# Tokens and w1 loaded in a set order, sixteen query buffers for the final tiles, squares kept in PSUM, fifth-group shifts on VectorE, another list order

## The chip, the cores and the metric

The kernel runs on one core of a Trainium2 chip. The metric is the device time of one execution in microseconds (us). Before the change three executions took 253.4, 253.51 and 253.84 us. The first part of the profile names the engines: PE is the matrix engine (TensorE), PEld its weight loads, which overlap it (94% and 57% of the span in before), DVE the VectorE, ACT the ScalarE, POOL the GpSimd, and SP the engine that here only issues transfers. The span of a profile is about 1.8 us shorter than the time of the same execution. Every execution here is the time of one core.

## The reference, cut to what matters

```python
S, D, F = 2048, 640, 1536
# A: short convolution of k, product with v, long convolution over the tokens, product with q
kv = shift_conv(k, shift_k) * v
y  = irfft(rfft(pad(kv)) * rfft(pad(ssm_k)))[:S] + kv * ssm_D
a  = q * y
# B: two MLPs on x = q, the first with shifts of four channel groups by +1, -1, +2, -2 tokens
h  = gelu(layernorm(x) @ w1)          # "mm1"
hs = shift_groups(h) @ w2             # "mm2"
x1 = x + hs
b  = x1 + gelu(layernorm(x1) @ w3) @ w4   # "mm3", "mm4"
g  = sigmoid((x * gate_w).sum(-1))
out = g * a + (1 - g) * b
```

Tokens are handled in 16 tiles of 128. The kernel computes the long convolution with matmuls and elementwise products (`unit`, `combine`, `final`); the products are DVE's main load.

## The kernel before

All operations are first recorded in a list, then placed in order by a list scheduler when the kernel is built, and then emitted engine by engine. Each engine works through its own list in order. The priorities are shifted by a table of some 340 constants found by search; another table gives other lists. Because helpers record the operations, many instructions share one line of source: here `L1021` is nearly every matmul, `L1002` DVE's two-input products and sums, `L1007` the one-input ones with scalars, `L1012` ACT. These are the parts that matter.

```python
    const("w1")
    P.dma(sp, w1, B_w1.rearrange("(c p) f -> p c f", p=128), early=True)
    const("w1x")     # the four 32-column ends of w1's groups, gathered by ACT
    act(w1x.rearrange("p c (g q) -> p c g q", g=4), w1.rearrange("p c (g q) -> p c g q", g=4)[:, :, :, 128:160], ACTF.Copy)
    ...
    def ln_math(l, t):
        s = {f: st[l, f][:, t:t + 1] for f in range(6)}
        ts(s[4], s[0], s[0], D ** -2.0, ALU.mult, ALU.mult, eng="pool")
        ts(s[3], s[1], s[4], 1e-5, ALU.subtract, ALU.add, eng="pool")
        pool_pow(s[5], s[3], neghalf[:, t:t + 1])
        ts(s[2], s[0], 1.0 / D, None, ALU.mult, eng="pool")
    ...
    def mm1(sc, k=None):
        for ft in range(5):
            pr = ps(1, "mm1")[:, 0:n]
            mm(pr, ...)                       # ft == 4: the fifth group, from w1x
            if ft < 4:
                act(hT[:, ft, 2 + t0:2 + t0 + n], pr, ACTF.Gelu_apprx_tanh)
            else:
                for g in range(4):            # four shifted gelus on 32 partitions each
                    c0, q = 2 + SHIFT[g] + t0, slice(32 * g, 32 * (g + 1))
                    act(hT[q, 4, c0:c0 + n], pr[q], ACTF.Gelu_apprx_tanh)
    ...
    def mm2(t):
        ...
        act(X[:, t, :].rearrange("p (b n) -> p b n", b=2), pr, ACTF.Copy, accum=st[1, 0][:, t:t + 1])
        act(xn2[t % 2], X[:, t, :], ACTF.Square, scale=D ** -0.5, accum=st[1, 1][:, t:t + 1])
    def ln2(t):
        ln_math(1, t)
        ts(xn2[t % 2], X[:, t, :], ...)                       # normalise
        P.dma(sp, xt[...], xn2[t % 2], transpose=True)        # DMA transpose
    ...
    def final(hh, c, q, k):
        qt, gy, ab = qb[k % 3], gyb[k % 6], abb[k % 4]        # three query buffers
        P.dma(sp, qt, rows(A_q))
        act(qt[:, 0], qt[:, 0], ACTF.Copy, scale=gst[3][:, ts_:ts_ + 1])
        ...
        tt(gy, gy, qt, ALU.mult)
        tt(gy, gy, two(X), ALU.add)
        P.dma(sp, rows(out), gy)
```

Only the sum of the squares is wanted, so the square's elements are junk. But they are written into `xn2[t % 2]`, the buffer that the DMA transpose of two tiles earlier still reads.

Of the kernel before, what the change touches and what calls it, by code (L numbers as in the profile page):

```python
# [494 lines left out]
def bass_gated_mix__ssm_conv_h3__mixer_s_mlp__prompt_kernel(  # L495
# [36 lines left out]
    def ps(n, cls):  # L532
# [3 lines left out]
    BIASES = {'combine-0-1|dve': -407794.3,  # L536
     'combine-0-2|dve': -45893.4,
     'combine-0-3|dve': -300815.7,
     'combine-1-1|dve': 387348.8,
     'combine-1-2|dve': 105422.5,  # L540
     'combine-1-3|dve': 217575.6,
     'const-G|sp': 262450.7,
     'const-Rh|sp': 136620.7,
     'const-R|sp': 305660.3,
     'const-d|act': 212132.6,
     'const-esel|act': -74065.4,
     'const-gelu|act': 205074.8,
     'const-gsum|act': -162352.0,
     'const-gsum|pe': -204554.3,
     'const-gw|act': -345180.8,  # L550
     'const-id|act': 44971.2,
     'const-set|dve': 264773.9,
     'const-shk|sp': 548954.8,
     'const-taps|act': -347541.8,
     'const-taps|pe': 157141.2,
     'const-w1x|act': -118397.4,
     'const-w1|sp': 86861.3,
     'const-w2|sp': -203887.8,
     'const-warm|dve': 531209.6,
     'const-warm|pe': -474841.2,  # L560
     'final-0-0-0-6|act': 471334.1,
     'final-0-0-0-6|dve': 95864.6,
     'final-0-0-0-6|pe': -207210.8,
     'final-0-0-0-6|sp': 33107.2,
     'final-0-0-1-7|act': 502462.3,
     'final-0-0-1-7|dve': -145429.9,
     'final-0-0-1-7|pe': -1657225.0,
     'final-0-0-1-7|sp': 36878.1,
     'final-0-1-0-4|act': -542556.9,
     'final-0-1-0-4|dve': 90833.3,  # L570
     'final-0-1-0-4|pe': -17806.8,
     'final-0-1-0-4|sp': 180740.8,
     'final-0-1-1-5|act': 162211.6,
     'final-0-1-1-5|dve': 299763.8,
     'final-0-1-1-5|pe': 53865.8,
     'final-0-1-1-5|sp': 517150.6,
     'final-0-2-0-2|act': 48931.5,
     'final-0-2-0-2|dve': 237254.9,
     'final-0-2-0-2|pe': 74789.6,
     'final-0-2-0-2|sp': 187724.9,  # L580
     'final-0-2-1-3|act': -58044.8,
     'final-0-2-1-3|dve': -198209.5,
     'final-0-2-1-3|pe': -447313.6,
     'final-0-2-1-3|sp': -178044.8,
     'final-0-3-0-0|act': -70783.7,
     'final-0-3-0-0|dve': 107510.8,
     'final-0-3-0-0|pe': -417546.4,
     'final-0-3-0-0|sp': 12746.7,
     'final-0-3-1-1|act': -75347.7,
     'final-0-3-1-1|dve': 217341.1,  # L590
     'final-0-3-1-1|pe': 46063.4,
     'final-0-3-1-1|sp': 295314.0,
     'final-1-0-0-14|act': 545361.7,
     'final-1-0-0-14|dve': -299052.3,
     'final-1-0-0-14|pe': -547102.0,
     'final-1-0-0-14|sp': -128720.9,
     'final-1-0-1-15|act': 283548.0,
     'final-1-0-1-15|dve': 287063.5,
     'final-1-0-1-15|pe': 74100.7,
     'final-1-0-1-15|sp': 55218.8,  # L600
     'final-1-1-0-12|act': 75127.8,
     'final-1-1-0-12|dve': 225694.6,
     'final-1-1-0-12|pe': -32443.2,
     'final-1-1-0-12|sp': 271002.4,
     'final-1-1-1-13|act': -378541.6,
     'final-1-1-1-13|dve': 60153.4,
     'final-1-1-1-13|pe': -4036185.1,
     'final-1-1-1-13|sp': -631105.6,
     'final-1-2-0-10|act': -55974.0,
     'final-1-2-0-10|dve': 51404.3,  # L610
     'final-1-2-0-10|pe': -1881219.8,
     'final-1-2-0-10|sp': 107741.8,
     'final-1-2-1-11|act': 24136.8,
     'final-1-2-1-11|dve': 51566.4,
     'final-1-2-1-11|pe': 130287.3,
     'final-1-2-1-11|sp': 52505.2,
     'final-1-3-0-8|act': -186216.5,
     'final-1-3-0-8|dve': 209149.2,
     'final-1-3-0-8|pe': -92431.9,
     'final-1-3-0-8|sp': -234054.7,  # L620
     'final-1-3-1-9|act': 328185.7,
     'final-1-3-1-9|dve': 118940.0,
     'final-1-3-1-9|pe': 182235.6,
     'final-1-3-1-9|sp': 183596.6,
     'gate|act': 43517.7,
     'gate|pool': -106208.4,
     'h_chunk-0|act': -159010.0,
     'h_chunk-0|pe': -40842.3,
     'h_chunk-1|act': 400527.7,
     'h_chunk-1|pe': 579587.5,  # L630
     'h_chunk-2|act': 221955.9,
     'h_chunk-2|pe': -278173.1,
     'h_chunk-3|act': -142551.9,
     'h_chunk-3|pe': -95219.8,
     'h_chunk-4|act': -295038.4,
     'h_chunk-4|pe': -117699.7,
     'h_fold-0|act': -43635.4,
     'h_fold-0|dve': -182917.2,
     'h_fold-0|sp': 128933.9,
     'h_fold-1|act': 131439.2,  # L640
     'h_fold-1|dve': -106402.2,
     'h_fold-1|sp': 76238.2,
     'h_fold-2|act': 54189.3,
     'h_fold-2|dve': 10793.0,
     'h_fold-2|sp': 183656.1,
     'h_fold-3|act': -176689.9,
     'h_fold-3|dve': -178738.7,
     'h_fold-3|sp': 510928.9,
     'h_fold-4|act': -169023.8,
     'h_fold-4|dve': 297432.5,  # L650
     'h_fold-4|sp': -174960.5,
     'h_load-0|sp': 509674.0,
     'h_load-1|sp': 167622.4,
     'h_load-2|sp': 13065.6,
     'h_load-3|sp': -76450.5,
     'h_load-4|sp': -69693.6,
     'kv_block-0-0|act': -236465.6,
     'kv_block-0-0|dve': -155765.4,
     'kv_block-0-0|pe': -216177.4,
     'kv_block-0-0|sp': 24500.6,  # L660
     'kv_block-0-1|act': 170890.0,
     'kv_block-0-1|dve': -229659.6,
     'kv_block-0-1|pe': 43906.6,
     'kv_block-0-1|sp': 205152.3,
     'kv_block-0-2|act': 125536.7,
     'kv_block-0-2|dve': -356717.8,
     'kv_block-0-2|pe': 79125.3,
     'kv_block-0-2|sp': 171049.0,
     'kv_block-0-3|act': 70834.6,
     'kv_block-0-3|dve': -219421.9,  # L670
     'kv_block-0-3|pe': 33243.5,
     'kv_block-0-3|sp': 114498.1,
     'kv_block-1-0|act': -172843.4,
     'kv_block-1-0|dve': -88259.4,
     'kv_block-1-0|pe': 310482.8,
     'kv_block-1-0|sp': 94105.8,
     'kv_block-1-1|act': -189736.4,
     'kv_block-1-1|dve': -311893.1,
     'kv_block-1-1|pe': 420317.8,
     'kv_block-1-1|sp': -113999.1,  # L680
     'kv_block-1-2|act': 257985.6,
     'kv_block-1-2|dve': 265069.2,
     'kv_block-1-2|pe': -186714.4,
     'kv_block-1-2|sp': -188963.0,
     'kv_block-1-3|act': -77752.5,
     'kv_block-1-3|dve': 217795.5,
     'kv_block-1-3|pe': -171943.0,
     'kv_block-1-3|sp': -97522.0,
     'ln1-0-1|act': -229928.8,
     'ln1-0-1|dve': 338936.6,  # L690
     'ln1-0-1|pe': -122227.5,
     'ln1-0-1|pool': -277023.9,
     'ln1-1-2|act': -121291.7,
     'ln1-1-2|dve': 34755.1,
     'ln1-1-2|pe': -464286.9,
     'ln1-1-2|pool': -2789.2,
     'ln1-10-12|dve': 135278.3,
     'ln1-10-12|pool': -82370.4,
     'ln1-10-12|sp': -519951.2,
     'ln1-12-14|dve': -149131.9,  # L700
     'ln1-12-14|pool': -189370.6,
     'ln1-12-14|sp': 129838.2,
     'ln1-14-16|dve': -273427.8,
     'ln1-14-16|pool': 348966.8,
     'ln1-14-16|sp': 511015.6,
     'ln1-2-3|act': 96809.9,
     'ln1-2-3|dve': 22463.4,
     'ln1-2-3|pe': -57286.1,
     'ln1-2-3|pool': -278158.0,
     'ln1-3-4|act': -17404.0,  # L710
     'ln1-3-4|dve': -2033735.8,
     'ln1-3-4|pe': -35392.7,
     'ln1-3-4|pool': 516069.5,
     'ln1-4-6|act': 23443.4,
     'ln1-4-6|dve': 371099.5,
     'ln1-4-6|pe': -141280.2,
     'ln1-4-6|pool': -37793.4,
     'ln1-6-8|act': 12616.8,
     'ln1-6-8|dve': 165383.0,
     'ln1-6-8|pe': 116177.6,  # L720
     'ln1-6-8|pool': -295203.5,
     'ln1-8-10|dve': -783165.6,
     'ln1-8-10|pool': 537697.9,
     'ln1-8-10|sp': -103863.4,
     'ln2-0|dve': 438689.5,
     'ln2-0|pool': 86456.1,
     'ln2-0|sp': 58318.2,
     'ln2-10|dve': -21795.2,
     'ln2-10|pool': -278895.9,
     'ln2-10|sp': -615162.9,  # L730
     'ln2-11|dve': 57754.3,
     'ln2-11|pool': -184196.2,
     'ln2-11|sp': 147086.4,
     'ln2-12|dve': -51938.1,
     'ln2-12|pool': -156601.3,
     'ln2-12|sp': -509388.8,
     'ln2-13|dve': 850852.2,
     'ln2-13|pool': -139798.1,
     'ln2-13|sp': 135197.4,
     'ln2-14|dve': 230784.7,  # L740
     'ln2-14|pool': -86117.4,
     'ln2-14|sp': 23549.2,
     'ln2-15|dve': -232737.1,
     'ln2-15|pool': 384762.2,
     'ln2-15|sp': 223053.3,
     'ln2-1|dve': -307987.6,
     'ln2-1|pool': 231749.2,
# [694 lines left out]
```

## Time and profile before

| | before |
|---|---|
| median of 3 runs | 253.51 us |
| span of the profiled execution | 250.5 us |
| PE, DVE busy | 94%, 89% of the span |
| first matmul of mm1 | 13.46 us |
| tiles 2 and 3 of the tokens landed | 5.48 and 6.06 us |
| w1 issued, landed | 4.12, 12.92 us |
| PE's last matmul ends | about 244.2 us |

Three lines of the page of before: its first part (busy us, share of the span, instructions), the clock granted to PE in 40 slices of the span (in tenths), and the chain of waits that ended last, by engine.

```profile
PE 236.6 (94%) x1564; PEld 143.4 (57%) x1564; DVE 223.0 (89%) x337; ACT 171.9 (69%) x327; POOL 73.0 (29%) x94
PEclk9999999999999999999999999999999999999998
PE 44%; DVE 17%; ACT 14%; DMA 11%; POOL 9%; issue 3%; SPq 1%; DVEq 0%; ACTq 0%; POOLq 0%
```

PE and DVE are both near the length of the span, PE is granted full speed up to the last slice (mean clock 0.996; in the clock's records half speed begins at 248.4 us), and the chain runs over PE most of the time.

The chain of waits of before between 119 and 134 us (start, us, what) shows a loop:

```profile
119.40 2.57 DMA arena<-arena
...
122.05 0.84 ACT arena L1012 x2
...
122.98 1.12 POOL arena L1007
...
124.17 1.66 POOL arena L1187
...
125.85 0.45 DVE arena L1007
...
126.33 2.67 DMA arena<-arena
...
129.08 0.84 ACT arena L1012 x2
```

A transpose ends, then the square that had to wait for its buffer runs, then POOL computes the power, DVE normalises, and the next transpose starts: seven microseconds a round, for a value that has nothing to do with the transpose.

From the groups of instructions by form of before (count, busy us, mean ns, idle time before and who ended it): the squares (with the w1x copy), the shifted gelus on 32 partitions, and POOL's statistics.

```profile
L1012 ACT ACTIVATE arena<-arena 128x640 bf16<-128x640 bf16 x17 | 12.6, 742 | 11.5 <-DMA arena<-arena 11.5
L1012 ACT ACTIVATE arena<-PSall 32x256 bf16<-32x256 f32 x16 | 6.0, 376 | 0.4 <-PE PSall L1021 0.2
L1012 ACT ACTIVATE arena<-PSall 32x512 bf16<-32x512 f32 x8 | 4.7, 589 | 0.1
L1007 POOL TENSOR_SCALAR arena<-arena 128x1 f32<-128x1 f32 x52 | 43.5, 839 | 48.0 <-ACT arena L1012 38.6 <-DVE arena L1184 7.3
```

ACT waits 11.5 us in all for transposes. A 128x1 operation of POOL takes 839 ns on average.

The timeline of PE of before, at the start (start, us, then what): twenty transposes, of the first four tiles of the tokens, come before mm1's first matmul.

```profile
11.16 1.84 PE L1228 MATMUL PSall<-arena 128*128 128x128 bf16 x20
13.46 6.11 PE L1021 MATMUL PSall<-arena 128*128 128x256 bf16 x70 [0.46 <-ACT arena L1012]
```

The timeline of SP of before at the end:

```profile
243.78 0.37 SPq L230 DMA_DIRECT2D arena<-in_A_q_dram  x1
```

The last query is loaded when PE is nearly done, since a buffer comes free only then.

To say where PE loses time I counted in each trace the columns that its matmuls move, divided them by 2,400 per us (a round figure just above the densest issue in these traces, 512 columns every 0.214 to 0.216 us) and took that from the time that went by. The count does not depend on how the profile models a matmul's end. The whole kernel moves 224.1 us' worth. In before 7.5 us are lost up to 30 us, 5.7 from there to 120, 3.8 between 120 and 150, 2.0 up to 240, and 7.4 after that.

### The profile page before, as it was taken

How to read it: one execution, taken by the hardware profiler on the slowest of the kernel's cores; microseconds unless marked ns; L12 is line 12 of the kernel's file. 1: busy time of each engine (PE TensorE's matmuls, PEld its weight loads, DVE VectorE, ACT ScalarE, POOL GpSimd, SP SyncE). 2: the span in 40 equal slices, each digit the busy share in tenths (PEclk: the TensorE clock that was granted, in tenths of full speed). 3: DMA queues.
4: the chain of work that ended last, by engine and by line, in shares of the span. 5: the costliest groups of instructions: out<-in, count | busy, mean ns of one | idle time of the engine just before them, and what ended most of it. 6: DMA issues, size and time to landing. Idle time of an engine off the chain costs nothing.

```text
span 250.5 us, 4194 instructions
## 1 busy us (share of the span) xinstructions
PE 236.6 (94%) x1564; PEld 143.4 (57%) x1564; DVE 223.0 (89%) x337; ACT 171.9 (69%) x327; POOL 73.0 (29%) x94
## 2 busy tenths in 40 slices
PE   7999999999999999999997979999999999999990
PEld 2488765455654575544474634676467645777750
DVE  5678889849999998898988899999999999998685
ACT  2699996999788999797724572236622286727993
POOL 1433199302460028855686722000000000000000
PEclk9999999999999999999999999999999999999998
DMA  6999999987799996596522210000000000303676
GB/s 141 366 275 274 286 220 231 229 183 208 118 236 263 293 244 161 132 309 137 141 38 43 52 26 3 0 13 16 0 0 3 1 0 3 106 0 104 167 198 188
DMA packets 59336, 33.87 MB, mean 135 GB/s; under 512 B 30136, under 2 KB 57652, under 8 KB 59316
## 3 DMA queue, kind: packets, MB, share of 16 engines
q1 hardware_dynamic: 57852, 33.50, 54.6%
q10 hardware_dynamic: 1464, 0.11, 0.4%
q8 instruction: 12, 0.20, 0.3%
q14 instruction: 8, 0.07, 0.1%
HBM read 24.42 MB, written 2.62 MB: 108 GB/s over the span
## 4 chain that ended last, share of the span: by engine, by line
PE 44%; DVE 17%; ACT 14%; DMA 11%; POOL 9%; issue 3%; SPq 1%; DVEq 0%; ACTq 0%; POOLq 0%
PE PSall L1021 43%; DVE arena L1002 15%; ACT arena L1012 14%; DMA arena<-arena 8%; POOL arena L1007 7%; DMA arena<-in_A_ssm_k_dram 2%; POOL arena L1187 2%; DVE arena L1007 1%; DMA arena<-in_A_q_dram 1%; SPq L230 1%; PE PSall L1228 1%; DVEq L443 0%; ACTq L443 0%; DVEq L441 0%; POOLq L441 0%
## 5 line engine op out<-in xcount | busy, mean ns | idle before, releaser
L1021 PE MATMUL PSall<-arena 128*128 128x320 bf16 (+4 forms) x1495 | 225.9, 311 | 5.9 <-ACT arena L1012 4.6
L1002 DVE TENSOR_TENSOR arena<-arena 128x640 bf16<-128x640 bf16 (+5 forms) x235 | 195.5, 881 | 13.2 <-ACT arena L1012 7.9
L1021 PEld LDWEIGHTS PSall<-arena 128*128 128x128 bf16 (+1 forms) x1495 | 138.4, 98 | 93.4 <-ACT arena L1012 9.6
L1012 ACT ACTIVATE arena<-PSall 128x640 bf16<-128x640 f32 (+8 forms) x206 | 121.5, 645 | 26.4 <-PE PSall L1021 21.6
L1007 POOL TENSOR_SCALAR arena<-arena 128x1 f32<-128x1 f32 (+2 forms) x61 | 46.2, 761 | 59.2 <-ACT arena L1012 39.7
L1012 ACT ACTIVATE arena<-arena 128x640 bf16<-128x640 bf16 (+4 forms) x55 | 34.5, 629 | 29.6 <-DVE arena L1002 15.8
L1012 ACT ACTIVATE arena<-PSall,arena 128x640 bf16<-128x640 f32 (+1 forms) x32 | 20.4, 660 | 16.8 <-PE PSall L1021 16.7
L1187 POOL TENSOR_TENSOR arena<-arena 128x1 f32<-128x1 f32 (+1 forms) x26 | 25.5, 984 | 1.6
L1007 DVE TENSOR_SCALAR arena<-arena 128x640 bf16<-128x640 bf16 (+1 forms) x37 | 14.5, 404 | 6.6 <-POOL arena L1187 6.2
L1183 DVE BATCH_NORM_STATS2 arena<-arena 128x6 f32<-128x320 bf16 x32 | 13.6, 476 | 3.9 <-DMA arena<-in_A_q_dram 3.9
L1047 PE MATMUL PSall<-arena 128*128 128x512 bf16 x24 | 7.9, 492 | 1.6 <-DVE arena L1043 1.6
L1002 POOL TENSOR_TENSOR arena<-arena 128x16 f32<-128x16 f32 x3 | 1.3, 447 | 18.0 <-DVE arena L1007 18.0
L1047 PEld LDWEIGHTS PSall<-arena 128*128 128x128 bf16 x24 | 2.7, 121 | 5.7 <-issue 3.2
L1228 PE MATMUL PSall<-arena 128*128 128x128 bf16 x40 | 3.2, 220 | 0.2
L1012 ACT ACTIVATION_READ_ACCUMULATOR arena<-PSall 128x1 f32 x16 | 3.3, 208 | 0.0
L1012 ACT ACTIVATION_READ_ACCUMULATOR arena<-arena 128x1 f32 x16 | 3.1, 195 | 0.0
L1050 ACT ACT_TABLE_LOAD x1 | 1.3, 1283 | 2.4 <-issue 2.4
L1228 PEld LDWEIGHTS PSall<-arena 128*128 128x128 bf16 x40 | 2.3, 97 | 1.0 <-DVE arena L1183 0.4
L1184 DVE BATCH_NORM_AGGREGATE arena<-arena 128x2 f32<-128x12 f32 x16 | 2.8, 196 | 0.0
L1043 DVE MEMSET arena<- 128x640 bf16 x1 | 0.6, 592 | 0.9 <-PEq L1427 0.9
L1141 DVE MEMSET arena<- 32x480 uint32 x2 | 0.9, 458 | 0.1
L1007 DVE TENSOR_SCALAR arena<-PSall 128x4 f32<-128x4 f32 x4 | 0.6, 146 | 0.1
(16 smaller groups left out, 2.0 us busy)
## 6 DMA issues: line engine op xcount, KB each, us to landing
arena<-in_A_k_dram SPq DMA_DIRECT2D x14, 400.0 KB, 4.6
arena<-in_A_q_dram SPq DMA_DIRECT2D x20, 160.0 KB, 2.9
arena<-in_A_ssm_k_dram SPq DMA_DIRECT2D x5, 512.0 KB, 5.5
arena<-in_A_v_dram SPq DMA_DIRECT2D x16, 160.0 KB, 3.6
out_dram<-arena SPq DMA_DIRECT2D x16, 160.0 KB, 2.4
arena<-in_A_q_dram SPq DMA_DIRECT2D x6, 320.0 KB, 9.2
arena<-in_B_w_dram SPq DMA_DIRECT2D x1, 1920.0 KB, 8.4
arena<-in_B_w_dram SPq DMA_DIRECT2D x1, 1152.0 KB
```

The lines of the kernel that those rows point to most:

```text
L230: fn = lambda e: e.dma_start(out, in_, **kw)
L1002: P.op(eng, lambda e: e.tensor_tensor(o, a, b, op), [a, b], [o], dve_ns(o, [a, b], 2) if eng == "dve" else 500)
L1007: P.op(eng, lambda e: e.tensor_scalar(o, real(a), s1, s2, op0=op0, **({} if op1 is None else {"op1": op1})), [a] + aps, [o], dve_ns(o, [a] ...
L1012: P.op("act", lambda e: e.activation(o, real(a), f, bias=bias, scale=scale, **({"accum_out": accum} if accum is not None else {})), [a] + ...
L1021: fns.append(lambda e, l=l, r=r, i=i: e.matmul(real(o), l, r, start=(i == 0), stop=(i == last)))
L1047: P.op("pe", [lambda e: e.matmul(real(pw), warm[:, 0:128], warm[:, 128:640], start=True, stop=True)] * 2, [warm], [pw], 856.0 if i < 4 els ...
L1050: P.op("act", lambda e: e.activation(tjunk[:, 1:2], ones[:, 0:1], ACTF.Gelu_apprx_tanh), [ones[:, 0:1]], [tjunk[:, 1:2]], 1700)
L1141: P.op("dve", lambda e: e.memset(kt[0:32, 0:3, :], 0.0), [], [kt[0:32, 0:3, :]], 500)
L1183: P.op("dve", lambda e, o=o, i=i: e.bn_stats(o, i), [i], [o], 400)
L1184: P.op("dve", lambda e: e.bn_aggr(bna[:, t, :], bns[k]), [bns[k]], [bna[:, t, :]], 120)
L1187: P.op("pool", lambda g: g.tensor_tensor(o, a, e, ALU.pow), [a, e], [o], 450 + 400 * n_of(o))
L1228: P.op("pe", [lambda e, c=c, pb=pb, xn=xn: e.transpose(real(pb)[:, 128 * c:128 * (c + 1)], xn[:, 128 * c:128 * (c + 1)], ident) for c in r ...
```

## The change

The intent is to take away the three losses: mm1's late start, the loop between squares and transposes, and the tail. The core of the diff (the table of priorities, some 370 lines, is cut):

```diff
     const("w1")
-    P.dma(sp, w1, ..., early=True)
+    P.dma(sp, w1, ..., bias=8e8, early=True)
     const("w1x")
-    act(w1x.rearrange("p c (g q) -> p c g q", g=4), w1.rearrange("p c (g q) -> p c g q", g=4)[:, :, :, 128:160], ACTF.Copy)
+    for g in range(4):
+        P.dma(sp, w1x[:, :, 32 * g:32 * (g + 1)], B_w1.rearrange("(c p) (g f) -> p c g f", p=128, g=4)[:, :, g, 128:160], bias=7.5e8, early=True)
     const("w2")                                   # likewise, bias 5e8 and 4e8
 ...
     def ln_math(l, t):
-        ts(s[4], s[0], s[0], D ** -2.0, ALU.mult, ALU.mult, eng="pool")
-        ts(s[3], s[1], s[4], 1e-5, ALU.subtract, ALU.add, eng="pool")
+        ts(s[2], s[0], 1.0 / D, None, ALU.mult, eng="pool")
+        ts(s[4], s[2], s[2], 1e-5, ALU.mult, ALU.subtract, eng="pool")
+        ts(s[3], s[1], s[4], None, ALU.subtract)            # on DVE
         pool_pow(s[5], s[3], neghalf[:, t:t + 1])
-        ts(s[2], s[0], 1.0 / D, None, ALU.mult, eng="pool")
 ...
-                P.dma(sp, X[:, i, :], A_q[0, 128 * i:128 * (i + 1), :], early=True)
+                P.dma(sp, X[:, i, :], A_q[0, 128 * i:128 * (i + 1), :], bias=(1e9, 9e8, 7e8, 6e8)[i], early=True)
 ...
             else:
+                hx = hxb[(2 * sc + (k or 0)) % 2][:, 0:n]
+                act(hx, pr, ACTF.Gelu_apprx_tanh)           # one gelu on 128 partitions
                 for g in range(4):
-                    act(hT[q, 4, c0:c0 + n], pr[q], ACTF.Gelu_apprx_tanh)
+                    P.op("dve", lambda e, o=hT[q, 4, c0:c0 + n], i=hx[q, :]: e.tensor_scalar(o, i, 1.0, None, op0=ALU.mult), ...)
 ...
-        act(xn2[t % 2], X[:, t, :], ACTF.Square, scale=D ** -0.5, accum=st[1, 1][:, t:t + 1])
+        act(pr, pr, ACTF.Square, scale=D ** -0.5, accum=st[1, 1][:, t:t + 1])
 ...
-        qt, gy, ab = qb[k % 3], gyb[k % 6], abb[k % 4]
+        qt, gy, ab = qb[k], gyb[k % 8], abb[k % 4]
 ...                                               # the last two tiles end in two halves
+        for e in ((0, 2),) if k < 14 else ((0, 1), (1, 2)):
 ...                                               # sixteen query buffers in oHF, free by then
-    BIASES = {...}
+    BIASES = {...}                                # other priorities: other list order
```

SP now issues, by these biases: tiles 0 and 1 of the tokens, w1, the four transfers of w1x, tiles 2 and 3, tiles 4 to 7, w2.

## The prediction

> **What bounds the kernel now.** By the first part of the page, over a span of 250.5 us, PE is busy 236.6 us (94%), DVE 223.0 (89%), ACT 171.9, POOL 73.0. Two engines limit it together: in the table of windows both are at or near 100% from 160 to 230 us. Counting the matmuls' moving columns in the trace, all but the warm-up makes 522 thousand; at the rate of the dense stretches (37 matmuls of 320 columns in 5 us) that is about 221 us, 224 with the small ones. So PE loses some 26 us, at three places:
> - start: mm1, which waits for tokens, w1 and w1x, starts at 13.5 us;
> - middle, 120 to 150 us: PE idles about 3 us. The chain of waits loops there: ACT square, POOL 1.1 to 2.9 us, POOL power 0.57, DVE 0.45, DMA transpose 2.6, back to ACT, since the square writes the buffer that the transpose reads. ACT waits 11.5 us in all for transposes;
> - tail: PE's last matmul ends near 244.2 us. The last query load is issued at 243.8, because only three query buffers exist, and takes 2.7 us; then scale, multiply, add, store.
>
> **Removed.** The squares' wait for transposes (they go to PSUM). From ACT: 24 shifted gelus on 32 partitions (10.7 us) and the w1x copy (0.7). From the tail: query loads and query scalings (0.56 each), which can run long before. From POOL's path after the square: all but the power. POOL ops stretch to 2.9 us while DVE runs two 1.44 us products[...].
>
> **Added or moved.** Six gelus on ACT (+2.8 us; net ACT -8.6). On DVE: 24 shifts, estimated 0.20 us (256 wide) and 0.28 us (512 wide) from its fixed cost of 0.11 to 0.15 us: 5.4 us; 16 subtractions of 128x1, 0.15 each: 2.4 us; the split of the last two tiles, 0.6 us. DVE grows about 8 us to 231, which eats a good part of the gain; it fits because most additions fall before 110 us, where DVE has idle time (about 5 us before 40 us, 4.4 from 40 to 60).
>
> **On the critical path.** Start: w1 is issued third instead of ninth; mm1 should begin at 10 to 11 us. But the taps and transposes done before it must still be done, and early mm1 is paced by ACT and DVE: net 1 to 2 us. Middle: 1 to 3 us, limited by DVE. Tail: 2 to 3 us (ACT per final falls from 1.8 to 1.25 us). The list order may win or lose 1 us. Sum about 7 us.
>
> **Predicted:** 246.5 us, 8 in 10 between 241.5 and 250.5. Faster by over 2%: 0.66; within 2%: 0.31; slower: 0.03.
>
> **What would show it right.** First mm1 matmul near 10.5 us. No wait of ACT for transposes. DVE busy 229 to 233 us, ACT 161 to 166. No query load after 230 us; at most 6 us from PE's last matmul to the end. DVE at least 94% of the span.
>
> **What would make it wrong.** The early order may leave new gaps on PE between 9 and 25 us (PE waits for ACT). Squares hold PSUM banks 1 us longer, so mm2 may wait. DVE waiting in order for the fifth gelu or POOL's power would put its 8 us fully on the path: then 249 to 251. If idle time is filled better than I think, 241.

What before's trace shows is this: POOL's three longest operations took 2.88, 2.62 and 2.44 us, at 130.0, 115.6 and 137.6 us, and each ended 0.08 to 0.17 us after the second of two long DVE products that ran meanwhile (1.48 to 1.49 us each). What DVE's "fixed cost" stands for is the time of its shortest arithmetic operations there: 0.109 us on four columns, 0.145 to 0.165 us on one.

## The result and the profile after

All ratios in this document are the mean time of one kernel's fast runs over the mean of the fast runs of before in the same rounds, with a 95% interval; they are not quite the ratio of the medians quoted with them.

| | before | after |
|---|---|---|
| median of 4 runs | 253.68 us | 250.38 us (250.05 to 251.09) |
| ratio | | 0.9875 (0.985 to 0.9899) |
| span of the profiled execution | 250.5 us | 248.6 us |
| first matmul of mm1 | 13.46 us | 11.18 us |
| tiles 2 and 3 landed | 5.48, 6.06 us | 10.65, 11.10 us |
| w2 landed | 19.5 us | 17.98 us |
| PE's last matmul to the end | about 6.3 us | about 5.2 us |

The gain is 3.2 us, where seven were forecast: the same within 2%. The same three lines of the page, of after:

```profile
PE 236.0 (95%) x1554; PEld 144.9 (58%) x1564; DVE 227.3 (91%) x381; ACT 163.2 (66%) x308; POOL 42.4 (17%) x74
PEclk9997999999999999999999999999999999999998
DVE 64%; PE 13%; issue 7%; ACT 5%; SPq 4%; DMA 2%; POOL 2%; DVEq 0%
```

ACT lost 8.7 us of work and DVE gained only 4.3. The chain went from PE to DVE. Two new things stand in these lines: the fourth slice of the clock is 7, and SP's queue has 4% of the chain. (Ten matmul records are missing from this trace.)

The chain of waits of after up to 23 us names what held the start:

```profile
2.13 0.53 SPq L230
...
2.69 0.70 SPq L230
...
3.44 1.42 SPq L230
...
4.89 3.21 SPq L230
...
12.17 5.81 DMA arena<-in_B_w_dram
...
18.07 4.53 PE PSall L1021 x22
```

The first four are the issues of the four w1x transfers, 0.53, 0.70, 1.42 and 3.21 us. SP's other issues before 14 us take 0.40 to 0.52. In SP's own timeline of after one sees what stands behind them:

```profile
1.65 6.46 SPq L230 DMA_DIRECT2D arena<-in_B_w_dram  x5
8.15 1.99 SPq L230 DMA_DIRECT2D arena<-in_A_q_dram  x4
10.19 2.41 SPq L230 DMA_DIRECT2D arena<-in_B_w_dram  x5
```

The five issues from 1.65 us on are w1 and w1x; tiles 2 to 7 of the tokens follow only at 8.15 us and w2 at 10.19. In before tiles 2 and 3 were issued at 1.66 and 2.13.

PE's timeline of after:

```profile
11.18 2.90 PE L1021 MATMUL PSall<-arena 128*128 128x256 bf16 x25 [0.25 <-ACT arena L1011]
15.56 0.81 PE L1229 MATMUL PSall<-arena 128*128 128x128 bf16 x10 [1.48 <-DVE arena L1006]
18.07 4.53 PE L1021 MATMUL PSall<-arena 128*128 128x320 bf16 x22 [1.71 <-DMA arena<-in_B_w_dram]
```

mm1 for tiles 0 and 1 starts early, as intended, and is done at 14.1 us. Then PE waits 1.5 us for DVE to normalise tiles 2 and 3, whose tokens are late, and then 1.7 us for w2. (Of the first wait e1 below still has 1.1 us: late tokens are the smaller part.) From 14.1 to 18.1 us it does 0.8 us of transposes. After that its 22 matmuls take 4.53 us.

The table of windows of after, from 12 to 24 us (window, length, then busy us and count of PE, PEld, DVE, ACT and POOL, granted clock, DMA share, GB/s):

```profile
12.00:18.00 6.00, 2.89 (x30) 2.18 (x27) 5.24 (x18) 3.15 (x7) 1.12 (x3) 1.00 1.06 316
18.00:24.00 6.00, 5.92 (x37) 3.95 (x38) 5.40 (x19) 2.53 (x7) 2.53 (x8) 0.72 1.10 341
```

PE "busy" 5.92 us in the second window is a slow PE: the granted clock is 0.72. The clock's records show half speed for 3.413 us from about 18.0 us on. The profiled run of before had none of this before 248.4 us, in its last slice.

The groups by form of after that answer to those of before:

```profile
L1011 ACT ACTIVATE PSall<-PSall 128x640 f32<-128x640 f32 x16 | 11.1, 696 | 0.2
L1251 DVE TENSOR_SCALAR arena<-arena 32x256 bf16<-32x256 bf16 x16 | 3.6, 223 | 0.3
L1251 DVE TENSOR_SCALAR arena<-arena 32x512 bf16<-32x512 bf16 x8 | 2.3, 287 | 0.2
L1006 DVE TENSOR_SCALAR arena<-arena 128x1 f32<-128x1 f32 x16 | 3.0, 206 | 2.1 <-POOL arena L1006 2.0
L1006 POOL TENSOR_SCALAR arena<-arena 128x1 f32<-128x1 f32 x32 | 17.0, 534 | 32.4 <-ACT arena L1011 30.5
```

The squares no longer wait for transposes. The shifts cost DVE 5.9 us, the subtractions 3.0. POOL's 128x1 operations are down to 32 of 534 ns.

### The profile page after: what moved, and what is told of

Read it like the earlier page. It is cut to its first block, busy times and chain, and to the rows that moved or that the text cites. A ratio compares the mean times of both kernels' runs of the same rounds, so it can differ in the third digit from the quotient of the medians.

```text
span 248.6 us, 4194 instructions
## 1 busy us (share of the span) xinstructions
PE 236.0 (95%) x1554; PEld 144.9 (58%) x1564; DVE 227.3 (91%) x381; ACT 163.2 (66%) x308; POOL 42.4 (17%) x74
## 3 DMA queue, kind: packets, MB, share of 16 engines
HBM read 24.58 MB, written 2.62 MB: 109 GB/s over the span
## 4 chain that ended last, share of the span: by engine, by line
DVE 64%; PE 13%; issue 7%; ACT 5%; SPq 4%; DMA 2%; POOL 2%; DVEq 0%
DVE arena L1001 60%; PE PSall L1021 13%; SPq L230 4%; ACT arena L1011 4%; DVE arena L1006 3%; DMA arena<-in_B_w_dram 2%; ACT PSall L1011 1%; POOL arena L1006 1%; POOL arena L1001 1%; DVE arena L1251 1%; DVE arena L1184 1%; POOL arena L1188 0%; DVE arena L1142 0%; DVEq L1419 0%; PE PSall L1078 0%
## 5 line engine op out<-in xcount | busy, mean ns | idle before, releaser
L1021 PE MATMUL PSall<-arena 128*128 128x320 bf16 (+3 forms) x1485 | 225.5, 312 | 3.7 <-DMA arena<-in_B_w_dram 1.7
L1001 DVE TENSOR_TENSOR arena<-arena 128x2560 bf16<-128x2560 bf16 (+5 forms) x239 | 192.3, 862 | 3.5 <-ACT arena L1011 2.7
L1021 PEld LDWEIGHTS PSall<-arena 128*128 128x128 bf16 x1495 | 139.5, 98 | 89.2 <-ACT arena L1011 1.9
L1011 ACT ACTIVATE arena<-PSall 128x640 bf16<-128x640 f32 (+5 forms) x188 | 113.8, 663 | 37.0 <-PE PSall L1021 27.4
L1006 POOL TENSOR_SCALAR arena<-arena 128x1 f32<-128x1 f32 (+2 forms) x43 | 19.8, 469 | 51.9 <-ACT arena L1011 30.5
L1011 ACT ACTIVATE arena<-arena 1x320 bf16<-1x320 bf16 (+3 forms) x38 | 20.7, 573 | 4.3 <-DVE arena L1001 1.9
L1006 DVE TENSOR_SCALAR arena<-arena 128x640 bf16<-128x640 bf16 (+2 forms) x53 | 17.0, 342 | 6.0 <-DMA arena<-arena 2.0
L1188 POOL TENSOR_TENSOR arena<-arena 128x1 f32<-128x1 f32 (+1 forms) x24 | 20.3, 854 | 4.8 <-DVE arena L1006 4.3
L1011 ACT ACTIVATE PSall<-PSall 128x640 f32<-128x640 f32 x16 | 11.1, 696 | 0.2
L1047 PEld LDWEIGHTS PSall<-arena 128*128 128x128 bf16 x24 | 2.9, 126 | 6.7 <-issue 3.6
L1251 DVE TENSOR_SCALAR arena<-arena 32x256 bf16<-32x256 bf16 (+1 forms) x24 | 5.9, 244 | 0.5
L1229 PEld LDWEIGHTS PSall<-arena 128*128 128x128 bf16 x40 | 2.4, 97 | 2.1 <-DVE arena L1006 1.8
```

The lines of the kernel that those rows point to most:

```text
L1001: P.op(eng, lambda e: e.tensor_tensor(o, a, b, op), [a, b], [o], dve_ns(o, [a, b], 2) if eng == "dve" else 500)
L1006: P.op(eng, lambda e: e.tensor_scalar(o, real(a), s1, s2, op0=op0, **({} if op1 is None else {"op1": op1})), [a] + aps, [o], dve_ns(o, [a] ...
L1011: P.op("act", lambda e: e.activation(real(o), real(a), f, bias=bias, scale=scale, **({"accum_out": accum} if accum is not None else {})), ...
L1021: fns.append(lambda e, l=l, r=r, i=i: e.matmul(real(o), l, r, start=(i == 0), stop=(i == last)))
L1047: P.op("pe", [lambda e: e.matmul(real(pw), warm[:, 0:128], warm[:, 128:640], start=True, stop=True)] * 2, [warm], [pw], 856.0 if i < 4 els ...
L1188: P.op("pool", lambda g: g.tensor_tensor(o, a, e, ALU.pow), [a, e], [o], dur)
```

## The experiments

**How they were made.** A change of one part would let the scheduler find other lists for everything. So I recorded, from the build of before and of after, the order of every engine's list and the place of every PSUM tile, and built the experiments by replaying that order, with only the named operations changed or moved. Replaying it with nothing changed gives the same lists. The price: a part taken alone has to live in an order tuned for the whole, so the effects of parts do not add up.

**The theories.** A, mine: the w1x transfers hold SP and the tokens and w2 that come late behind them cost PE two waits and then the half clock; without them the forecast would have come true. B, the rival: DVE, with its added work, now sets the time from about 100 us on, so what happens at the start costs nothing and the missing gain was eaten by DVE's additions. B has the chain of waits on its side: in after it runs over DVE, nearly without a break, from 104.4 to 245.9 us.

All kernels gave correct results. `e` and `f`, `g`, `h`, `i` are partly on different chips; each ratio is against before on the same chip.

| run | base | part changed | median us | ratio (95%) |
|---|---|---|---|---|
| e1_w1x_act | after | w1x by ACT again | 246.76 | 0.9719 (0.9671 to 0.9767) |
| e2_w1x_actq | after | w1x transfers on ACT's queue | 255.12 | 1.0035 (0.9974 to 1.0096) |
| e3_tokens_first | after | tokens before w1 | 250.87 | 0.9883 (0.9829 to 0.9938) |
| e4_act_and_tokens | after | e1 and e3 | 247.52 | 0.9765 (0.9702 to 0.9828) |
| f4_start | after | e4, start mended | 248.98 | 0.9782 (0.9734 to 0.983) |
| h1_start2 | after | f4, flaw mended | 246.71 | 0.973 (0.9674 to 0.9786) |
| h2_fill | after | useless matmuls in PE's gaps | 248.48 | 0.9785 (0.976 to 0.9811) |
| f1_shift_act | e1 | shifts on ACT again | 251.58 | 0.9887 (0.9844 to 0.9929) |
| g1_before_squares | before | squares in PSUM alone | 252.32 | 0.9916 (0.9874 to 0.9958) |
| g2_before_ln | before | new ln_math alone | 257.01 | 1.0119 (1.0074 to 1.0164) |
| g3_before_queries | before | query buffers, first try | 286.66 | 1.1251 (1.1195 to 1.1307) |
| g4_before_queries2 | before | query buffers alone | 253.12 | 0.9978 (0.9931 to 1.0025) |
| i0_after | after | nothing (control) | 251.12 | 0.99 (0.986 to 0.9941) |
| i1_best | after | e1 again | 246.86 | 0.9759 (0.9731 to 0.9786) |
| i2_more_dve | e1 | 1.44 us more on DVE | 248.26 | 0.9811 (0.9784 to 0.9838) |
| i3_more_pe | e1 | 1.49 us more on PE | 249.01 | 0.9839 (0.9799 to 0.9879) |

### e1: w1x by ACT again

```diff
-    for g in range(4):
-        P.dma(sp, w1x[:, :, 32 * g:32 * (g + 1)], ... [:, :, g, 128:160], bias=7.5e8, early=True)
+    act(w1x.rearrange(...), w1.rearrange(...)[:, :, :, 128:160], ACTF.Copy)   # first on ACT, before the tokens' evictions
```

> The kernel after, with one part undone in the same frozen order on every engine: w1x is again copied from w1 by ACT (about 0.74 us, while ACT is idle near 9 us) and its four DMAs of 64-byte pieces are gone from SP. Theory A (start): those DMAs hold SP from 2.1 to 8.2 us, so tokens 2 and 3 and w2 come late, PE starves from 14.1 to 18.1 us and is then given half clock for 3.4 us. Then tokens 2 and 3 land near 8.5 us instead of 10.7 and 11.1, w2 about 2 to 3 us earlier than 18.0, the half-clock stretch near 18 us shrinks or goes, and the time falls 1.5 to 4 us to 246.5 to 249. Rival B (DVE): DVE, fully busy from 120 to 240 us with the work that the change gave it, sets the end whatever PE does at the start: PE's gap shrinks, but the time falls by less than 0.8 us.

It took 246.76 us (246.09 to 247.24), by the ratio 7.1 us less than before, where after had won 3.2. This is theory A's result. The page of this run, the same three lines:

```profile
PE 234.1 (96%) x1564; PEld 144.1 (59%) x1564; DVE 227.1 (93%) x381; ACT 164.3 (67%) x309; POOL 43.4 (18%) x74
PEclk9999999999999999999999999999999999999997
DVE 67%; PE 14%; issue 8%; ACT 5%; POOL 4%; DVEq 0%
```

DVE's work is the same as in after, 227.1 us, and the time is shorter: DVE's additions cannot be what was missing. The clock is full again until PE's work is done, and SP's queue is gone from the chain. The timeline of SP of this run:

```profile
1.65 0.43 SPq L230 DMA_DIRECT2D arena<-in_B_w_dram  x1
2.13 2.32 SPq L230 DMA_DIRECT2D arena<-in_A_q_dram  x4
4.49 2.65 SPq L230 DMA_DIRECT2D arena<-in_B_w_dram  x5
```

And the timeline of its PE:

```profile
10.29 2.90 PE L1021 MATMUL PSall<-arena 128*128 128x256 bf16 x25 [0.25 <-ACT arena L1011]
14.28 0.81 PE L1229 MATMUL PSall<-arena 128*128 128x128 bf16 x10 [1.08 <-DVE arena L1006]
15.35 2.90 PE L1021 MATMUL PSall<-arena 128*128 128x320 bf16 x22 [0.27 <-DVE arena L1251]
```

The tokens and w2 are issued 6 us earlier; tiles 2 and 3 land about 2 us earlier (8.68 and 9.25 us) and w2 4 us (14.00). The same 22 matmuls that took 4.53 us in after start 2.7 us earlier and take 2.90.

What the pieces do to the transfers shows in the view of DMA between 8.0 and 9.3 us. The first line is of after:

```profile
DMA packets 959, 0.06 MB, mean 46 GB/s; under 512 B 959, under 2 KB 959, under 8 KB 959
```

The same line, over the same stretch, of this run:

```profile
DMA packets 519, 0.43 MB, mean 329 GB/s; under 512 B 185, under 2 KB 519, under 8 KB 519
```

A w1x transfer is 640 pieces of 64 bytes. While they run, 46 GB/s are moved in place of 329. Part of that is an idle queue: SP had issued nothing else, and the same view gives the transfer engines of after as 49.7% busy there. Per piece the busy time works out at 10.8 ns for 64 bytes in after (49.7% of 16 engines for 1.3 us, 959 pieces) and at 60 ns for 1,200 bytes in e1 (102.3%, 356 pieces). So a piece of 19 times the size kept an engine busy only about 5.5 times as long.

### e2: the w1x transfers on ACT's queue

```diff
-        P.dma(sp, w1x[...], ...)
+        P.dma("act", w1x[...], ...)
```

> The kernel after, the four w1x DMAs issued by ACT's queue instead of SP's, right after the gate weights; same bytes and same 64-byte pieces, frozen order otherwise. If it is the blocking of SP's issue that costs, tokens 2 and 3 land 1.5 to 2.5 us earlier, as in the run with the ACT copy, and the time falls by as much (1.5 to 4 us), unless ACT is itself held past 9.8 us. If it is the traffic of the small pieces on the DMA engines, tokens 2 and 3 stay near 10.5 us and the time stays at 250 to 251. Rival B: within 0.8 us of 250.4 in either case.

It took 255.12 us, 0.35% over before: worse than after itself. SP was free and tiles 2 and 3 landed at 9.5 and 10.0 us, a microsecond earlier than in after. But the pieces of w1x now ran beside what SP had issued (the transfer engines' share is 1.15 from 12 to 18 us, 287 GB/s, and 1.11 from 18 to 24, 347 GB/s), and landed at 12.5, 15.2, 17.0 and 19.0 us (in after at 9.0 to 9.7). The list of waits of this run has

```profile
PE PSall L1021 <- DMA arena<-in_B_w_dram: 5.7, 1, 5.7
```

that is, one wait of 5.7 us, and the half clock then lasted 10.2 us (the granted clock is 0.89 from 12 to 18 us, 0.50 to 24 and 0.76 to 30). In this run another queue did not make 2,560 small pieces cheap. Their issue had held SP; on another queue their landing held PE.

### e3 and e4: tokens first

In e3 the order of SP alone was changed, tiles 2 and 3 before w1, w2 before tiles 4 to 7, with w1x still by transfers on SP; e4 has the same and w1x by ACT.

```diff
 SP's list:  tokens 0, tokens 1,
+            tokens 2, tokens 3,
             w1, w1x (4 transfers; e4: none),
-            tokens 2, tokens 3, tokens 4-5, tokens 6-7, w2
+            w2, tokens 4-5, tokens 6-7
```

> The kernel after, with SP's list changed at the start alone: tokens 2 and 3 before w1, and w2 before tokens 4 to 7; the w1x DMAs stay on SP. Theory A: tokens 2 and 3 land near 5.5 us, DVE normalises them 3 us earlier, w1 lands about 1 us later (9.5 us, still before PE needs it at 11.2); w2 still stands behind w1x and lands near 14 to 15. PE's gap from 14.1 to 18.1 us closes to under 1 us and no half clock follows: the time falls 2 to 4 us. Rival B: under 0.8 us.

> Both: w1x copied by ACT, and tokens 2 and 3 before w1, w2 before tokens 4 to 7. Theory A: the best of the four; w2 lands near 12 us, PE idles less than 1 us between 11 and 20 us, no half clock, and the time falls 3 to 5 us to 245.5 to 247.5. Rival B: 249.6 or more, with DVE's idle time moved from the start to the middle.

e3 was a miss: 250.87 us, no better than after. Tiles 2 and 3 landed at 5.28 and 6.31 us and w2 at 13.6, as wanted. But DVE's list takes the statistics of tiles 4 to 7 before it normalises tiles 2 and 3, and those tokens now landed at 14.5 and 15.4, so PE waited 2.7 us for DVE instead, and the half clock came back (0.72 from 18 to 24 us). Only the operation that waited had changed. With w1x by ACT (e4) the half clock was gone (the 22 matmuls took 2.90 us) and the time 247.52 us. It did not gain over e1: w1 landed later, at 9.01 us, and ACT did the w1x copy ahead of the tokens' evictions, so mm1 began at 11.01 us.

### h2: useless matmuls in PE's gaps

To separate the wait itself from the half clock that follows, after was given 21 matmuls whose result nobody uses, ten before and eleven after the transposes of tiles 2 and 3. The transfers are those of after.

```diff
         pr = ps(2, "mm2")[:, :, 0:320]
+        for n in (10, 11) if t == 0 else ():
+            P.op("pe", [lambda e: e.matmul(real(pr[:, 0, :]), w1[:, 0, 0:128], w1[:, 0, 128:448], start=True, stop=True)] * n, [w1], [pr[:, 0, :]], 0)
```

> The kernel after, nothing mended: 21 matmuls of 320 columns that compute nothing (w1 times w1, into the bank that the next real product overwrites) are put on PE into its two waits, 10 before and 11 after the transposes of tokens 2 and 3; they end before the data that PE waits for, so no real matmul starts later. If the half clock near 18 to 21.4 us is given because PE stood idle before it, it disappears, the 22 matmuls after it take about 2.9 us instead of 4.5, and the time falls 1 to 1.7 us below the 250.4 us of after. If the clock comes from something else, or DVE sets the time, it stays within 0.5 us of 250.4.

With more work for PE the kernel is faster: 248.48 us (248.29 to 248.83), a ratio of 0.9785 against 0.9875 for after. No half clock is left (1.00 from 12 to 24 us), and PE's timeline of this run shows the 22 matmuls at full speed:

```profile
15.65 1.66 PE L1273 MATMUL PSall<-arena 128*128 128x320 bf16 x11
17.14 2.88 PE L1021 MATMUL PSall<-arena 128*128 128x320 bf16 x22
```

So of the three to four microseconds between after and e1 one and a half to two are the clock: half speed for 3.413 us costs 1.7 by arithmetic, and the 22 matmuls took 1.65 less here than in after. The rest is the wait proper. One reservation: in this run the matmuls also began 0.9 us earlier than in the profiled run of after, because transfers landed a little earlier, so the split is rough.

What the traces show of the clock can be counted. In the records of after it is at half speed from 18.045 to 21.459 us, 3.413 us, and again from 246.7 us to the end, with 225.28 us at full speed between; in those of before from 248.4 us to the end alone. I cut both traces into stretches of 3.413 us that end where these changes lie, and counted in each the columns moved by matmuls that use all 128 rows and columns (the transposes included), as a share of the 8,192 that fit at 2,400 per us. Of the 143 stretches whose following clock is on record three have a share of 0.16 (after, from 14.6 us), 0.02 (after, from 243.3) and 0.00 (before, from 245.0), and were followed by half clock; the others have 0.43 or more and were followed by full clock. In h2 the stretch from 12.1 us has about 0.67, and full clock after it. PE's busy time does not tell as much: in f1 below PE was busy for 2.57 of the 3.41 us before 22.97 us, partly with matmuls of four rows or of a single moving column, and the clock was halved all the same. This is a count on this one kernel. How much work would have been enough was not tested.

### f4 and h1: is there more to win at the start?

```diff
-    WARM = 12
+    WARM = 10      # both: fewer warm-up matmuls, the tokens' first transposes earlier between them
 both: w1x by ACT, one place later than in e1; SP's order as in e4
 DVE's list:
+    normalise tiles 2 and 3     (f4: ahead of some, h1: ahead of all of the next line)
     statistics of tiles 4, 5, 6, 7
```

> On top of the ACT copy of w1x: the rest of the start mended in the frozen order. The warm-up tile is set first on DVE, transposes of tokens 0 and 1 stand after 16 warm-up matmuls (10 x 2 in all, two fewer pairs), tokens 2 and 3 come before w1 and w2 before tokens 4 to 7 on SP, the w1x copy stands after ACT's first two evictions, and DVE normalises tokens 2 and 3 before it touches tokens 4 to 7. If PE's first matmuls set the time, mm1 starts near 9.3 us instead of 10.3 and 11.2, tokens 2 and 3 are transposed by 13 us, PE's lost time before 30 us falls from 8.0 to about 6 us, and the time falls 1 to 2 us below the 246.76 us of the ACT copy. If DVE's own sum of work sets the time, PE's gain of the first 30 us reappears as idle PE between 30 and 120 us, and the time stays within 0.5 us of 246.76.

> The mended start again, with the flaw of the first try removed: there DVE stood in order before three statistics of tokens 4 to 7, waited 3.3 us for them and held up the normalising of tokens 2 and 3, so PE starved and was given half clock again. Now DVE normalises tokens 2 and 3 and makes the first shifts before any of tokens 4 to 7. Expected if PE's start sets the time: transposes of tokens 2 and 3 near 11.5 to 12 us, no half clock, PE's lost time before 30 us 6 to 7 us (8.0 with the ACT copy alone), and 0.8 to 1.8 us less than the ACT copy alone, a ratio to before of 0.964 to 0.969. If DVE's sum of work sets it: a ratio of 0.970 to 0.974.

f4 had a flaw of mine. mm1 began at 9.11 us, but DVE still stood 3.3 us at the statistics of later tiles, the transposes of tiles 2 and 3 came at 14.28 us, and the half clock was back (the 22 matmuls took 4.57 us): 248.98 us. h1 mended this. mm1 began at 9.59 us and the next stage at 13.92, 1.4 us before e1's 15.35, with no half clock (2.90 us for the 22 matmuls). It took 246.71 us: no gain over e1's 246.76 that these runs can show (other chip; ratios 0.973 and 0.9719, each uncertain by about 0.5%, so the low end of the forecast is not excluded). It met a new wait of 1.3 us at 22 us, and the stretch that the chain of waits spends on DVE, from 100.2 to 241.8 us, is as long as in after, 141.6 and 141.5 us. In e1 it is 141.5 us too and begins at 100.8: that it begins 3.6 us sooner than after's is e1's gain, and h1 made it begin only 0.6 us sooner still. This fits theory B for the remainder: what is won at the start counts only as far as it reaches the beginning of that stretch.

### f1: the shifts on ACT again

```diff
 # on top of e1
-                hx = hxb[...]; act(hx, pr, ACTF.Gelu_apprx_tanh)
                 for g in range(4):
-                    P.op("dve", ... e.tensor_scalar(o, i, 1.0, None, op0=ALU.mult) ...)
+                    act(hT[q, 4, c0:c0 + n], pr[q], ACTF.Gelu_apprx_tanh)
```

> On top of the ACT copy of w1x: the fifth-group shifts go back to ACT, as 24 gelus on 32 partitions, frozen order otherwise; the DVE copies are gone. DVE's busy time falls by about 5.9 us to 221, ACT's rises by about 8 to 172. If DVE, full from 120 to 240 us, is the limit, the time falls 1 to 5 us below 246.76. If the early mm1 stage, where ACT is full, sets the pace, PE waits for ACT more between 12 and 60 us and the time rises 1 to 4 us, which would say that the move to DVE paid for itself.

DVE's busy time fell from 227.1 to 221.5 us, and still the kernel took 251.58 us, about 4 us more than e1 by the ratios (0.9887 against 0.9719). The waits of this run:

```profile
DVE arena L1001 <- ACT arena L1011: 10.4, 8, 3.4
PE PSall L1021 <- ACT arena L1011: 4.5, 7, 1.0
```

In e1 the first of these was 2.4 us and PE's 0.5: with the shifts on ACT, DVE and PE wait for ACT. A half clock near 23 us came back as well (0.91 from 18 to 24 us; ten transposes from 23.77 us took 1.23 us, earlier ten 0.72) and is part of the loss. So the work moved to DVE pays for itself, where by theory B taking it away from DVE should have won time. The list order was tuned for the shifts on DVE, so the 4 us are what the move is worth in this order, not in every order.

### g1, g2, g3 and g4: parts of the change alone, in before

```diff
 # g1: in mm2
-        act(xn2[t % 2], X[:, t, :], ACTF.Square, scale=D ** -0.5, accum=...)
+        act(pr, pr, ACTF.Square, scale=D ** -0.5, accum=...)          # right after the eviction
 # g2: ln_math as in the change, nothing else
 # g3, g4: in final, sixteen query buffers and eight for the output
-        qt, gy, ab = qb[k % 3], gyb[k % 6], abb[k % 4]
+        qt, gy, ab = qb[k], gyb[k % 8], abb[k % 4]                    # loads and scalings before the tail
```

> The kernel before with one part of the change alone: squares are taken in place in PSUM, each right after its eviction on ACT; the lists of PE, DVE and SP are those of before. ACT's wait for DMA transposes (11.5 us) goes. If the loop of square and transpose was what held the middle, PE's lost time between 120 and 150 us falls from 3.8 us to 1 to 2 and the time falls 1 to 3 us. If DVE's list and its load hold the middle, the waits pass to DVE or POOL and the time falls by less than 0.6 us.

> The kernel before with the second normalisation's arithmetic alone as in after: mean and square of the mean on POOL ahead of the square, the subtraction on DVE in the place where POOL made it, power on POOL. The path from the square to the normalised tile loses one POOL operation (1 to 2.9 us) and gains a DVE operation of about 0.2 us. [...]If DVE stands in order waiting for the square now, the time rises or stays within 0.5 us.

The first case is cut here, since it named a mechanism that no run shows. Its forecast was: if POOL's long operations (up to 2.88 us in before) held the middle, PE's loss there falls by 1 us or more and the time by 0.5 to 2 us.

> The kernel before with another part alone: sixteen query buffers and eight output buffers, all query loads on SP after the last transpose and the sixteen scalings on ACT between 165 and 215 us; the other lists stay nearly as they are. If the late query loads make the tail, the time from PE's last matmul to the end falls from 6.3 to about 4 us, ACT's load after 230 us falls by some 5 us, and the time falls 1.5 to 3 us. If the tail is DVE's own work on the last tiles, it falls by less than 0.7 us.

> The part with sixteen query buffers alone on the kernel before, second try: in the first, recorded waits of transfers for other transfers were kept although the transfers had been moved, so that the inverse-transform table stood behind the queries and ACT waited 24.5 us for queries. They are dropped now, and the lists of PE, DVE and POOL are those of before word for word. If the late query loads make the tail, the end comes 1.5 to 3 us sooner and ACT is busy less after 230 us; if the tail is DVE's work on the last tiles, less than 0.7 us.

g1 won 0.84%, 2.1 us. PE's loss between 120 and 150 us fell from 3.76 to 0.27 us, so the loop was the cause of it. But between 30 and 120 us the loss rose from 5.7 to 8.7 us, with PE waiting 2.9 us for the squares in PSUM: there the banks are held longer, as the prediction had feared.

g2 lost 1.2%. A subtraction on DVE that waits for POOL and ACT, put into lists that were not ordered for it, delays DVE, whose waits for ACT rose from 7.9 to 11.4 us; PE's loss between 120 and 150 us rose to 4.40 us. About 1.7 us of the profiled run's loss is a half clock from 239.1 us on, after PE had waited 2.0 us for ACT (its mean clock is 0.986, before's 0.996). The part is of use only together with the squares in PSUM, if at all.

g3 was an error of mine. In the frozen order each transfer also kept the place behind the transfers that it had in before, so a table needed earlier stood behind the query loads, and ACT waited 24.5 us for queries. It says nothing about the change and was replaced by g4, where the tail's transfers are free of that. g4 took 253.12 us, 0.2% less than before with an interval that spans zero: about 0.5 us. (Its profiled run was its slowest, 255.11 us, with a mean clock of 0.988 where its others had 0.996 to 0.998, so its trace is not used.) The tail alone, in before's order of PE, DVE and POOL, is worth much less than the forecast's two to three.

### i0 to i3: control, the best version again, and which engine limits it

The last four ran on one chip with the same runs of before. i0 is after replayed, i1 is e1 again. i2 adds to e1 one useless DVE product of 1.44 us near 140 us; i3 adds seven useless matmuls of 512 columns, 1.49 us at 2,400 columns per us, near 175 us.

```diff
 # i2, in unit
+        if (hh, c) == (0, 2):
+            tt(T0, T1, T1, ALU.mult)
 # i3, in mm3
+            if (sc, ft) == (2, 11):
+                P.op("pe", [lambda e, pr=pr: e.matmul(real(pr), w3[0][:, 0:128], xt[:, 0, :], start=True, stop=True)] * 7, ...)
```

> The kernel after, unchanged, issued from its recorded order: a control, and the base of the next run on the same chip. Every engine's list is the same as in after. Expected 250.4 us, within 0.4%, a ratio to before of 0.985 to 0.990, and a stretch of half clock near 18 us in every run (mean granted clock 0.983 to 0.989).

> After with w1x copied by ACT, a second time, beside after on the same chip: whether the better version holds. Expected a ratio to before of 0.970 to 0.975 and 1.2 to 1.7% below after. A ratio above 0.98 would say that the first result was luck.

> The version with the ACT copy, with one useless product of 2560 columns (1.44 us) more on DVE near 140 us, its result overwritten unread. If DVE's list sets the end from 100 us on, as the chain of waits says, the time rises 1.1 to 1.6 us; if DVE only looks busy and PE sets the end, by less than 0.5 us.

> The same version, with seven useless matmuls of 512 columns (1.49 us) more on PE near 175 us, overwritten before they are read. PE is fully busy there and issues at its dense rate. If PE sets the end too, the time rises 1.1 to 1.6 us; if DVE alone sets it, by less than 0.5 us. Both rising would say that the two engines are balanced and that neither's list can be shortened alone.

The means of the fast runs are 250.6 us for i0 and 247.0 for i1: on one chip, side by side, undoing the w1x transfers is worth 3.6 us. PE's timelines of i0 and i1 differ by at most 0.05 us up to the transposes (15.24 and 15.20 us); then come the 22 matmuls, first of i0, then of i1:

```profile
18.21 4.54 PE L1021 MATMUL PSall<-arena 128*128 128x320 bf16 x22 [2.17 <-DVE arena L1184]
16.27 2.90 PE L1021 MATMUL PSall<-arena 128*128 128x320 bf16 x22 [0.27 <-DVE arena L1251]
```

They start 1.9 us later and take 1.6 us longer, 3.6 us in all. The first is the wait for w2, whose last piece landed at 18.12 us in i0 and at 14.80 in i1 (the view names DVE in i0, but DVE's shifts were done at 16.3 us in both); the second is the half clock (0.72 from 18 to 24 us in i0). The tokens of tiles 2 and 3, late in i0 as well, cost nothing here. One of i0's six runs took 248.41 us, with a mean clock of 0.994 where the others had 0.982 to 0.989: it seems to have escaped the half clock by chance, and lies where h2, which has none, lies. (One run of i0, at 252.82 us, was slow and is left out.)

The profiled run of i0 has all its matmul records, so the count of PE's lost time can be laid side by side (us; the parts sum to the span less 224.1):

| stretch of the span | before | i0 (after) | i1 (e1) |
|---|---|---|---|
| 0 to 30 us | 7.5 | 12.3 | 8.9 |
| 30 to 120 us | 5.7 | 6.0 | 4.6 |
| 120 to 150 us | 3.8 | 0.4 | 0.6 |
| 150 to 240 us | 2.0 | 1.6 | 1.9 |
| 240 us to the end | 7.4 | 5.5 | 5.1 |
| sum | 26.4 | 25.8 | 21.0 |

The profiled execution of before was its fastest, 252.32 us, over a microsecond under the timed ones, so its column is somewhat too good. (It had a mean clock of 0.996; the runs of before beside i0 to i3 had 0.984 to 0.995, so some of them may have met a half clock too. Their traces were not kept.) The table still shows where things went: after wins 3.4 us in the loop's stretch and 1.9 in the tail, and gives 4.8 back at the start. It also shows that mending w1x does not bring the start's forecast gain: up to 30 us i1 still loses 8.9 us and the profile of e1 8.0, where before loses 7.5. mm1 begins earlier, and PE loses the time again behind it. i1 comes within a microsecond of the forecast sum by the rest, 4.4 us between 30 and 240 us and 2.3 after that.

i2 rose by 1.3 us over i1 and i3 by 2.1 (means of fast runs; i3's four runs lie between 248.25 and 250.31 us, so the 2.1 is uncertain by about 1). Nearly all that is added to DVE, and all that is added to PE, shows in the time. The chain of waits by engine of i1 is

```profile
DVE 69%; PE 15%; issue 8%; ACT 5%; POOL 2%; DVEq 0%
```

and that of i3 is

```profile
PE 76%; DVE 15%; ACT 3%; issue 3%; POOL 2%; DVEq 0%; ACTq 0%
```

With 1.5 us more on PE the whole chain turns from DVE to PE. The two are balanced to within that; what the chain names is the one that is ahead by a little. After e1 neither the start nor one engine's load alone is left as an easy gain.

**Verdict.** Theory A stands as the cause of the miss: by undoing the w1x transfers alone e1 reaches the forecast's ratio of 0.972, and i1 comes within 0.4% of it, in sum though not term by term. Theory B falls as that cause, since DVE's load is equal in after and e1. With the start mended it is half right: DVE and PE then limit the kernel together (i2 and i3). The version of e1 and i1 beats both kernels: 0.9719 and 0.9759 of before.

Two things stay open. Why the issue of w1x's third and fourth transfers takes 1.42 and 3.21 us is not shown. In before, too, one issue, of 256 pieces of 1,280 bytes, took 1.98 us, with seven of SP's transfers still to land. And the parts of the change were not separated fully: g1, g2 and g4 measure them in before's order, and the new order of the lists was never measured by itself.

## Why the prediction was wrong, point by point

- **The step that failed: "Start: w1 is issued third instead of ninth; mm1 should begin at 10 to 11 us. ... net 1 to 2 us."** The first half held: mm1 began at 11.18 us in place of 13.46. The net was of the other sign: 4.7 to 4.8 us more lost up to 30 us. The transfers of w1x were read as a removed ACT copy of 0.7 us and not costed as 2,560 pieces of 64 bytes ahead of tiles 2 and 3 and w2. They hold SP until 8.15 us; PE then waits for w2 (1.9 us longer in i0 than in i1) and runs 3.4 us at half speed (1.6 us more for the same 22 matmuls). With them undone (e1, i1) the ratio is 0.9719 and 0.9759, where the forecast of 246.5 us is 0.972. A second part of the step failed too: even then PE loses 8.0 and 8.9 us up to 30 us, more than before's 7.5, so the earlier beginning of mm1 was no gain by itself. That the ratio still comes to or near the forecast is due to larger gains elsewhere, and so partly luck.
- **"The early order may leave new gaps on PE between 9 and 25 us (PE waits for ACT)."** The place was right and the reason wrong: PE waited for w2 and, mostly in e1 as well, for DVE. The half clock was not thought of at all.
- **Middle, "1 to 3 us, limited by DVE".** A little under-sized. From 30 to 240 us 11.4 us are lost in before and 8.0 in i0, a gain of 3.5; in the profile of after it is nearer 5 if the ten missing records are counted in (8.6 less 2.1). ACT's wait for transposes is gone, as foretold. The squares alone bring 2.1 us.
- **Tail, "2 to 3 us".** The mechanism was right: no query is loaded after 230 us, and PE's last matmul is followed by about 5 us, at most 6 as foretold. The size was high: 1.6 us in after's profile, 1.9 in i0's, and 0.5 for the buffers alone in before's order.
- **DVE "grows about 8 us to 231", busy 229 to 233.** It grew by 4.3 us to 227.3. The shifts took a little longer than estimated, 5.9 us against 5.4, and the subtractions 3.0 against 2.4. What was not foreseen is that DVE was busy 192.3 us with two-input operations in place of 195.5 though there are four more of them, which gave back part of the growth. Why stays open. That POOL works less beside them is not the reason as far as the largest go: in before the 128x2560 products take 1,487 ns on average with POOL at work beside them (28) and 1,490 without (52). ACT at 163.2 us was within the 161 to 166 foretold.
- **"DVE at least 94% of the span".** 91% in after and 93% in e1. The share was too high because the growth was.
- **List order, "may win or lose 1 us".** Not measured by itself.

With the start a loss of 4.8 us, the sum of the terms is a gain of 0.6 us between the profiles of before and i0 and 1.9 us between those of before and after, while the timed runs gave 3.2; the profile of before was its fastest run. The predicted range, 241.5 to 250.5 us, held the result at its upper edge.

## What to carry to other kernels

When a change replaces a small on-chip copy by transfers, count the pieces and look at what stands behind them in the issuing engine's list: here an issue that took 3.21 us delayed everything after it, and another queue did not help (e2, 255.12 us). When a stage that should begin earlier leaves PE idle for some microseconds, look at the granted clock after the gap, since the slow stretch that follows can cost nearly as much as the gap did (here 1.6 us after 1.9, i0 against i1). And an engine that the chain of waits names for 65% of the span may be ahead of another by no more than a microsecond or two (in i3 1.5 us more on PE turned the chain from 69% DVE to 76% PE); add a known amount of work to each to find out.
